# Moving the reload of filter pieces and the first six visits in a fused frequency-filter and feed-forward kernel

## The chip, the cores and the metric

The kernel runs on one core of a Trainium2 chip. The metric is the device time of one execution in microseconds. The engines named here are TensorE (PE in the profile; its weight loads are PEld), VectorE (DVE), ScalarE (ACT), GpSimd (POOL) and SyncE (SP). SP computes nothing; most transfers are issued from its queue (SPq), and the others, mainly loads of the input and of the filter, from GpSimd's.

## The reference

The input x has 8 batches of 3008 positions with 256 channels. The reference multiplies its spectrum along the positions by a complex filter, transforms back, and puts each of the 24064 rows through two matrices with a leaky ReLU between them:

```python
X = np.fft.rfft(x, axis=1)
F = (filt_r + 1j * filt_i)[None, :, :]
y = np.fft.irfft(X * F, n=x.shape[1], axis=1)
h = y.reshape(B * S, D) @ w_in        # 256 x 2048
out = np.maximum(0.01 * h, h) @ w_out # 2048 x 256
```

## The kernel before

**The transform.** 3008 is split as 94 x 32, so the Fourier transform and its inverse are four matmul stages per batch with a turn of the data between stages 1 and 2 (through the DRAM buffer dz1) and between stages 3 and 4 (through dz2). Stage 1 (`s1_group`, L283) makes 16 groups of 512 columns; pairs of them are stored to dz1 (L288) and read back turned (`t1_load`, L297, the z1 loads). Stage 2 transforms and multiplies by the filter; stage 3 transforms back; results are stored to dz2 and read back turned (`t2_load`, L307, the z2 loads); stage 4 (`sb_group`, L461) makes yt, the input of the feed-forward part.

**The filter multiply.** The product of spectrum and filter takes two multiplies by VectorE, one with fb (the imaginary part) and one with fa (the real part), a transfer on SP that exchanges halves or neighbouring partitions of the first product, and an addition on GpSimd. Batches 0 and 1 do it in one layout (`s2_group`, L337 to L352; stage 3 in `sa_group`, L359, with its dz2 store at L363). From batch 2 on (`QUARTERS = 2`) stages 2 and 3 run in tiles of 64 x 64 in so-called visits, six to a batch. A visit (`visit`) calls `forward` for its own part (L411 matmuls, then `filtered` twice, the second time 1.05 slots later: multiplies L421 and L425, two swap copies on SP L424, addition L427) and `backward` for the part of the visit before it (L435 matmuls, ACT copy L437, dz2 store L438). So the addition of one visit has to be done when the next one comes.

**The filter's second layout.** The visits need fa and fb in another order of partitions, so both are loaded again in three pieces by groups: piece 0 holds groups 0 to 11, piece 1 holds 12 to 17, piece 2 holds 18 to 23. A piece cannot be reloaded before batch 1 has used its old content (`when[2, 1, ...]` is the slot of that use). For each piece `refills` issues eight loads on GpSimd (L375, four of fb and four of fa), each filling every other partition, then two copies on SP that fill the neighbours (`both`, L382, fb first) and a sign multiply of fb on VectorE (`signed`, L386). A visit v from 0 to 5 reads groups 2v and 2v + 1 and also 12 + 2v and 13 + 2v: visit 0 needs pieces 0 and 1, visit 3 is the first to need piece 2.

**The feed-forward part.** The rows go in 47 chunks of 512. `moe1` makes the hidden layer of a chunk (L624, with the leaky ReLU on ACT at L629, eight times per chunk). From chunk 3 on the second matrix is applied in seven products instead of eight (`products`, L699), which needs sums on VectorE (L665) and additions of results (L727 to L763); rows are stored from SP (L685).

**Order.** All queues' orders are written out ahead of time. Time in the plan is counted in slots: chunk c takes the slots from 8c to 8c + 8, `at(slot, f)` puts an instruction's issue at a slot, and at the end everything is issued in order of slot. A slot sets only the order within each engine's queue; an engine whose next instruction waits for nothing goes ahead. `PLANS` gives for batches 1 to 4 (later ones repeat batch 4's, shifted) the first slot and step of stage 1, of stage 2, the lag of stage 3, the first slot and step of stage 4, and those of the x loads. A planner loop (L858 to L879) then places each stage's groups at least 0.6 slots apart, away from visits by `AROUND`, and not before their loads can have landed. `load_time` (L839) puts a z1 load at the latest of three: first use less `LEAD[0]` = 3.85 (first use is one slot before the batch's first visit), the end of stage 1 plus 0.53 + 2.43, and 0.1 after the visit that last read its buffer:

```python
loads[stage, b, c] = t = max(first_use[stage, b] - LEAD[stage // 2], place.get((stage, c % 4), 0),
                             when[end] + AFTER[4 * (stage // 2)] + LANDED)
```

In the plan before, batch 1's stage 2 has its groups 5, 8 and 11 at slots 19.67, 24.47 and 28.67, its stage 3 ends at 33.47, and the refills of pieces 0, 1 and 2 begin at 21.37, 26.17 and 46.5. The first four z2 loads of batch 1 are at 36.29, the first eight z1 loads of batch 2 at 40.03, stage 1 of batch 3 runs from 40.7 to 70.85, and the first eight z1 loads of batch 3 are at 73.81. A visit's first swap copies come 0.8 slots after it, the second ones 1.85; its additions are at 1.4 and 2.45.

Of the kernel before, what the change touches and what calls it, by code (L numbers as in the profile page):

```python
# [19 lines left out]
N1, N2 = 94, 32  # L20
# [64 lines left out]
def kernel(  # L85
# [29 lines left out]
    DUE = (3.52, 0.66)  # L115
    TWICE = (2.2, 2.35)
    QUARTERS = 2
    VISITS = (44.75, 49.75, 55.75, 60.75, 65.75, 71.75) + tuple(8 * c + 4.75 for c in range(9, 40))
    AROUND = (0.8, 1.15, 2.1)
    HOLDS = (1.0, 2.0)  # L120
    PAIRS = (0.35, 0.1, 0.1)
# [1 line left out]
    ADDED = 1.4  # L123
    STORED = 1.2
    REFILLED = 1.7
    LATE = 46.5
    F2T = 3.24
    LEAD = (3.85, 7.37)
    AFTER = (0.53, 0.8, 1.33, 3.17, 0.39, 0.52)
# [2 lines left out]
    PLANS = (  # L132
        (0.68, 0.31, 12.95, 0.9, 4.35, 38.33, 2.78, 7.78, 1.61),
        (12.19, 1.53, 42.87, 2.62, 7.4, 85.59, 2.85, 16.13, 2.12),
        (40.7, 1.93, 77.28, 3.57, 5.62, 130.03, 2.65, -0.23, 2.52),
        (63.95, 2.85, 119.86, 3.87, 7.04, 177.42, 2.92, 12.93, 2.24),
    )

# [14 lines left out]
    fa_sb = cpool.tile([P, NC, D], FP16, name="fa_sb")  # L153
    fb_sb = cpool.tile([P, NC, D], FP16, name="fb_sb")
# [38 lines left out]
    def at(time, f):  # L193
        clock["n"] += 1
        heapq.heappush(work, (time, clock["n"], f))
# [8 lines left out]
    def noted(what, f):  # L204
        f()
        issued.add(what)
# [148 lines left out]
    def sa_group(b, g):  # L355
        def go():
            ps = bank("pf", 2, D)
            need(("y", b, g), *[("st2", b, g // 2 - 4)] * (g > 7))
            nc.tensor.matmul(ps, inv2, ys.pop((b, g))[:], start=True, stop=True)  # L359
            h = g // 2  # L360
            nc.scalar.copy(st2[h % 4][:, ds(2 * (g % 2), 2), :], ps)
            if g % 2:
                soon(AFTER[4], lambda: noted(("st2", b, h), lambda: nc.sync.dma_start(  # L363
                    dz2[b % 2][ds(4 * h, 4)].rearrange("k p d -> p k d"), st2[h % 4])))
        return go
# [4 lines left out]
    def halves(v):  # L370
        return v.rearrange("(k e) j d -> e k j d", e=2)

    def refill(dst, src, q, par, k, first, sgn):
        lo = H * par + Q * k
        nc.gpsimd.dma_start(  # L375
            halves(dst[lo : lo + Q, q])[0],
            bass.AP(tensor=src.tensor, offset=src.offset + (first + sgn * (par + 2 * q.start)) * D,
                    ap=[[N1 * D, N2 // 2], [sgn * 2 * D, q.stop - q.start], [1, D]]))

    def both(t, q):  # L380
        v = halves(t[:, q])
        nc.sync.dma_start(v[1], v[0])  # L382

    def signed(q):
        v = fb_sb[:, q]
        nc.vector.tensor_scalar(v, v, sign_sb[:], None, AL.mult)  # L386

    def refills(q, t):
        for n in range(8):
            dst, src = ((fb_sb, filt_i), (fa_sb, filt_r))[n // 4]  # L390
            at(t + 0.4 * n, lambda v=(dst, src, q, n // 2 % 2, n % 2, *((0, 1), (N1, -1))[n % 2]): refill(*v))
        at(t + 4.2, lambda: both(fb_sb, q))
        at(t + 5.6, lambda: both(fa_sb, q))
        at(t + 7, lambda: signed(q))
        if q.start == 0:
            at(t, lambda: nc.sync.dma_start(sign_sb[:], sign_d.ap()))
        elif q.stop < NC:
            t = when[2, 1, 11] + REFILLED
            at(t, lambda: nc.sync.dma_start(i2q_sb[:], i2q_d.ap()))
            at(t, lambda: noted(("f2q",), lambda: nc.sync.dma_start(f2q, f2q_d.ap())))  # L400
# [403 lines left out]
    def plan(b, s1, s1_step, s2, s2_step, lag, sb, sb_step, xl, x_step):  # L804
# [5 lines left out]
        if b < QUARTERS:  # L810
            for g in range(12):
                groups.append((s2 + s2_step * g, 2, b, g, s2_group(b, g)))
                groups.append((s2 + lag + s2_step * g, 3, b, g, sa_group(b, g)))
        first_use[1, b], first_use[3, b] = s2 if b < QUARTERS else VISITS[6 * (b - QUARTERS)] - 1, sb
        for g in range(16):
# [33 lines left out]

    visits = VISITS[: 6 * (B - QUARTERS) + 1]  # L850
    for i, t in enumerate(visits):
# [8 lines left out]
    while queue:  # L860
        time, n, stage, b, g, f = heapq.heappop(queue)
        t = max(time, last + GAP)
        for v in visits:
            if -AROUND[0] < t - v < AROUND[1] or AROUND[1] < t - v < AROUND[2] and last > v:
                t = v + AROUND[1 if last < v else 2]
# [15 lines left out]
    for i, t in enumerate(visits):  # L881
        b, v = QUARTERS + i // 6, i % 6
# [2 lines left out]
            assert ready is not None and ready + READ < t, (b, v, ready, t)  # L885
            place[1, v % 4] = t + 0.1

    for lo, hi, t in ((0, 12, 0), (12, 18, 0), (18, 24, LATE)):
        refills(slice(lo, hi), max(t, when[2, 1, hi // 2 - 1] + REFILLED))

    later = {}
# [49 lines left out]
```

## Time and profile before

| | |
|---|---|
| median of 3 runs | 756.85 us (754.44 to 758.82) |
| profiled execution, its own time | 757.12 us |
| its span from first to last instruction | 755.3 us |
| TensorE busy | 736.3 us (97%) |
| ScalarE busy | 552.4 us (73%) |
| VectorE busy | 527.1 us (70%) |
| GpSimd busy | 180.8 us (24%) |
| mean granted TensorE clock | 0.993 |
| transfers | 117.23 MB, mean 155 GB/s |

The lines of the profile name the engine, the line of the kernel, the operation and its tiles (output, then inputs after the arrow, without buffer numbers). In a timeline the columns are start in us, length in us, engine, line, operation, tiles and forms, the number of instructions merged, and, in square brackets, how long the engine stood idle before and what released it. SPq lines are issues of transfers: their length is that of the issue, not of the transfer. In a table by stretches each engine's busy time is followed by its number of instructions, then come the granted clock (1.00 is full, 0.50 half speed), the mean busy share of the 16 DMA engines and their rate in GB/s.

### The profile page before, as it was taken

The numbers are of one execution on the slowest core, as the hardware profiler recorded it, in microseconds if no ns is written. First come the engines' busy times: TensorE is split into PE (matmuls) and PEld (weight loads), VectorE is DVE, ScalarE is ACT, GpSimd is POOL, SyncE is SP. The second block draws the span as 40 slices with busy tenths as digits, with TensorE's granted clock in tenths as the row PEclk, the third lists the DMA queues.
The fourth block names the chain that finished last, engine by engine and source line by source line (L and its number), as shares of the span: only waits on it lengthen the run. The fifth ranks groups of instructions, "written<-read, shape, count | busy, mean of one in ns | idle before, by whom it ended". The sixth has DMA issues, their size and how long they took to land.

```text
span 755.3 us, 19901 instructions
## 1 busy us (share of the span) xinstructions
PE 736.3 (97%) x8233; PEld 519.6 (69%) x8233; DVE 527.1 (70%) x689; ACT 552.4 (73%) x719; POOL 180.8 (24%) x195
## 2 busy tenths in 40 slices
PE   8999988989999999999999999999999999999997
PEld 3556656656677666777768766786777777777776
DVE  5977635656777777777766777677777778455466
ACT  4776775758877787778778778777777777776762
POOL 5504630433242222222223311221122131000000
PEclk9999999989999999999999999999999999999999
DMA  9997998886687548665576545643364322311012
GB/s 204 227 226 192 226 260 216 181 199 174 194 233 182 153 126 216 177 162 141 153 209 170 156 125 175 188 132 123 105 186 134 122 92 93 107 55 53 30 45 69
DMA packets 124794, 117.23 MB, mean 155 GB/s; under 512 B 17744, under 2 KB 97488, under 8 KB 124512
## 3 DMA queue, kind: packets, MB, share of 16 engines
q1 hardware_dynamic: 105913, 96.72, 41.8%
q0 software_dynamic: 18512, 19.06, 16.8%
q8 instruction: 64, 1.05, 0.6%
q10 hardware_dynamic: 279, 0.19, 0.1%
q14 instruction: 26, 0.21, 0.1%
HBM read 61.07 MB, written 50.33 MB: 147 GB/s over the span
## 4 chain that ended last, share of the span: by engine, by line
PE 91%; DMA 5%; DVE 1%; ACT 1%; issue 0%; POOL 0%; SPq 0%; POOLq 0%; DVEq 0%; ACTq 0%
PE ph L624 42%; PE pf L699 18%; PE po_ps L699 18%; PE pf L283 3%; PE pf L461 3%; PE pf L411 2%; DMA p_b_v<-p_b_v 2%; PE pf L791 1%; PE po_ps L791 1%; PE ph L435 1%; DMA dz<-big 1%; DMA big<-dz 1%; DMA fb_sb<-fb_sb 1%; DMA big<-in_x_dram 1%; PE po_ps L483 1%
## 5 line engine op out<-in xcount | busy, mean ns | idle before, releaser
L629 ACT ACTIVATE gt_c<-ph 128x1024 f16<-128x1024 f32 x376 | 384.9, 1024 | 156.5 <-PE ph L624 152.0
L624 PE MATMUL ph<-yt,w_in_sb 128*128 128x512 f16 (+7 forms) x1728 | 449.5, 353 | 0.2 <-ACT yt L451 0.2
L699 PEld LDWEIGHTS <-gt_c 128*128 128x128 f16 x2800 | 199.1, 98 | 94.3 <-DVE gt_c L665 2.1
L699 PEld LDWEIGHTS <-big 128*128 128x128 f16 x2128 | 146.5, 98 | 70.5 <-issue 14.1
L427 POOL TENSOR_TENSOR y_b_v<-p_b_v,p_b_v 128x512 f16<-128x512 f32 x72 | 103.0, 1431 | 380.8 <-DMA p_b_v<-p_b_v 209.5
L624 PEld LDWEIGHTS <-w_in_sb 128*128 128x128 f16 x1728 | 136.8, 98 | 17.0 <-issue 1.3
L699 PE MATMUL po_ps<-wt_sb,gt_c 128*128 128x128 f16 x704 | 69.2, 219 | 1.9 <-DVE gt_c L665 1.9
L665 DVE TENSOR_TENSOR gt_c<-gt_c 128x2048 f16<-128x2048 f16 x43 | 67.3, 1565 | 1.4
L699 PE MATMUL pf<-wt_sb,big 128*128 128x128 f16 x704 | 66.1, 221 | 1.6 <-DVE big L752 1.6
L699 PE MATMUL pf<-w_out_sb,gt_c 128*128 128x128 f16 x720 | 66.5, 219 | 0.0
L699 PE MATMUL pf<-wt_sb,gt_c 128*128 128x128 f16 x688 | 66.0, 219 | 0.0
L699 PE MATMUL po_ps<-w_out_sb,gt_c 128*128 128x128 f16 x688 | 65.0, 221 | 0.0
L665 DVE TENSOR_TENSOR big<-gt_c 128x2048 f16<-128x2048 f16 (+1 forms) x46 | 64.5, 1402 | 0.3
L286 ACT CAST big<-pf 128x512 f16<-128x512 f32 x98 | 57.0, 583 | 8.7 <-PE pf L283 7.6
L699 PE MATMUL po_ps<-wt_sb,big 128*128 128x128 f16 x688 | 62.9, 219 | 0.0
L451 ACT CAST yt<-pf 128x376 f16<-128x376 f32 x120 | 56.2, 471 | 7.9 <-PE pf L461 5.0
L665 DVE TENSOR_TENSOR big<-big,gt_c 128x2048 f16<-128x2048 f16 (+1 forms) x45 | 56.2, 1249 | 0.1
L421 DVE TENSOR_TENSOR p_b_v<-pf,fb_sb 128x512 f32<-128x512 f32 x72 | 49.3, 685 | 7.7 <-PE pf L411 4.2
L665 DVE TENSOR_TENSOR big<-gt_c,big 128x2048 f16<-128x2048 f16 (+1 forms) x45 | 54.0, 1201 | 0.0
L425 DVE TENSOR_TENSOR p_b_v<-pf,fa_sb 128x512 f32<-128x512 f32 x72 | 48.9, 680 | 0.0
L283 PE MATMUL pf<-x_sb,small_sb 94*128 94x512 f16 x109 | 41.5, 381 | 0.0
L461 PE MATMUL pf<-i_sb,big 96*128 96x94 f16 x448 | 38.4, 207 | 2.4 <-DMA big<-dz 2.4
(108 smaller groups left out, 637.4 us busy)
## 6 DMA issues: line engine op xcount, KB each, us to landing
dz<-big SPq DMA_DIRECT2D x98, 256.0 KB
p_b_v<-p_b_v SPq DMA_DIRECT2D x144, 128.0 KB
out_dram<-ost_c_h SPq DMA_DIRECT2D x118, 128.0 KB
big<-dz SPq DMA_DIRECT2D x56, 192.0 KB
big<-dz SPq DMA_DIRECT2D x72, 128.0 KB
x_sb<-in_x_dram POOLq DMA_DIRECT2D x40, 192.0 KB, 4.8
x_sb<-in_x_dram POOLq DMA_DIRECT2D x2, 768.0 KB, 8.7
big<-dz SPq DMA_DIRECT2D x6, 256.0 KB
```

Of the source, the lines that this page charges most:

```text
L283: nc.tensor.matmul(ps, fwd1[:N1], x_sb[:N1, ds(2 * g, 2), :], start=True, stop=True)
L286: copy(st[:, ds(2 * (g % 2), 2), :], ps)
L411: nc.tensor.matmul(ps[s][ts(par, H), j, :], f2q[ts(s, H), 4 * v + c, :], z1[v % 4][ts(s, H), c, :], start=True, stop=True)
L421: nc.vector.tensor_tensor(p2[:], ps, fb2[:, s, ds(2 * v, 2), :], AL.mult)
L425: nc.vector.tensor_tensor(p1[:], ps, fa2[:, s, ds(2 * v, 2), :], AL.mult)
L427: soon(ADDED, lambda: noted(("yq", b, v, s), lambda: nc.gpsimd.tensor_tensor(y[:], p1[:], p3[:], AL.add)))
L451: copy(yv, ps.rearrange("p c a -> p a c"))
L461: nc.tensor.matmul(ps[:, j, :], z2[h % 4][:K4, j, ts(dt, P)], i1_sb[:K4, 4 * h + j, :], start=True, stop=True)
L624: nc.tensor.matmul(ph[:, j, ds(t - ci * CH, e - t)], w_in_sb[:, dt, ts(ct, P)], yt[:, dt, ds(t % N, e - t)], start=(dt == 0), stop=(dt == ...
L629: nc.scalar.activation(gts[ci][:, ds(2 * g, 2), :], ph, AF.Lrelu)
L665: nc.vector.tensor_tensor(*(v[:, ds(c0, n)] for v in (o, i0, i1)), op)
L699: nc.tensor.matmul(of[t], a()[:, c, ts(t, P)], w[:, c, :], start=(c == 0), stop=(c == NCH - 1))
```

## The change

Four things change, all in the order of work; no instruction is added or taken out.

- `LATE` becomes a tuple with an earliest slot for each of the three filter pieces: 0, 35.5 and 45, where only piece 2 had one, 46.5.
- In `refills` the eight loads of a piece are 0.6 slots apart instead of 0.4, and the two copies and the sign multiply come 7, 8.2 and 11 slots after the first load instead of 4.2, 5.6 and 7.
- The first six visits (batch 2) move from 44.75, 49.75, 55.75, 60.75, 65.75 and 71.75 to 48.75, 53.75, 57.75, 62.75, 67.75 and 71.75. The seventh stays at 76.75.
- The step of batch 3's stage 1 goes from 1.93 to 1.73 slots.

```diff
-    VISITS = (44.75, 49.75, 55.75, 60.75, 65.75, 71.75) + tuple(8 * c + 4.75 for c in range(9, 40))
+    VISITS = (48.75, 53.75, 57.75, 62.75, 67.75, 71.75) + tuple(8 * c + 4.75 for c in range(9, 40))
...
-    LATE = 46.5
+    LATE = (0, 35.5, 45)
...
-        (40.7, 1.93, 77.28, 3.57, 5.62, 130.03, 2.65, -0.23, 2.52),
+        (40.7, 1.73, 77.28, 3.57, 5.62, 130.03, 2.65, -0.23, 2.52),
...
-            at(t + 0.4 * n, lambda v=(dst, src, q, n // 2 % 2, n % 2, *((0, 1), (N1, -1))[n % 2]): refill(*v))
-        at(t + 4.2, lambda: both(fb_sb, q))
-        at(t + 5.6, lambda: both(fa_sb, q))
-        at(t + 7, lambda: signed(q))
+            at(t + 0.6 * n, lambda v=(dst, src, q, n // 2 % 2, n % 2, *((0, 1), (N1, -1))[n % 2]): refill(*v))
+        at(t + 7, lambda: both(fb_sb, q))
+        at(t + 8.2, lambda: both(fa_sb, q))
+        at(t + 11, lambda: signed(q))
...
-    for lo, hi, t in ((0, 12, 0), (12, 18, 0), (18, 24, LATE)):
+    for lo, hi, t in zip((0, 12, 18), (12, 18, 24), LATE):
         refills(slice(lo, hi), max(t, when[2, 1, hi // 2 - 1] + REFILLED))
```

## The prediction

> **What bounds the kernel now.** I read the page's engine rows first, then TensorE's timeline for its idle gaps, then the timelines of VectorE, the DMA queue SP and GpSimd at those gaps, and last a table by stretches for the clock.
>
> ```profile
> PE 736.3 (97%) x8233; PEld 519.6 (69%) x8233; DVE 527.1 (70%) x689; ACT 552.4 (73%) x719; POOL 180.8 (24%) x195
> ```
>
> TensorE is the bound: 97% busy, next 73%. A change that leaves its matmuls alone, as this one does, can move only its idle time and its half-clock time. After the first 35 us TensorE has six gaps over 0.3 us:
>
> ```profile
> 97.49 0.38 PE L359 MATMUL pf<-y_b_g,small_sb 128*128 128x512 f16 x1 [0.48 <-POOL y_b_g L352]
> 101.29 0.38 PE L359 MATMUL pf<-y_b_g,small_sb 128*128 128x512 f16 x1 [0.59 <-POOL y_b_g L352]
> 106.89 0.23 PE L699 MATMUL po_ps<-wt_sb,gt_c 128*128 128x128 f16 x1 [1.95 <-DVE gt_c L665]
> 115.57 0.35 PE L461 MATMUL pf<-i_sb,big 96*128 96x94 f16 x4 [2.36 <-DMA big<-dz]
> 149.72 0.27 PE L699 MATMUL pf<-wt_sb,big 128*128 128x128 f16 x2 [1.62 <-DVE big L752]
> 155.16 0.64 PE L435 MATMUL ph<-y_b_v,i2q_sb 64*64 64x512 f16 x3 [3.14 <-POOL y_b_v L427]
> ```
>
> They add up to 10.14 us, all between 97 and 156 us, the time of filter pieces 1 and 2 and of the first visits. Why they arise stands in the other engines' timelines (VectorE, then SP, then GpSimd):
>
> ```profile
> 105.08 0.62 DVE L386 TENSOR_SCALAR fb_sb<-fb_sb,sign_sb 128x1536 f16<-128x1536 f16 x1 [5.41 <-DMA fb_sb<-fb_sb]
> 148.09 0.97 DVE L386 TENSOR_SCALAR fb_sb<-fb_sb,sign_sb 128x1536 f16<-128x1536 f16 x1 [3.29 <-DMA fb_sb<-fb_sb]
> ```
> ```profile
> 98.60 0.49 SPq L382 DMA_DIRECT2D fb_sb<-fb_sb  x1
> 105.49 1.03 SPq L363 DMA_DIRECT2D dz<-big  x1
> 112.31 1.74 SPq L307 DMA_DIRECT2D big<-dz  x4
> 144.75 0.47 SPq L382 DMA_DIRECT2D fb_sb<-fb_sb  x1
> 148.37 1.17 SPq L424 DMA_DIRECT2D p_b_v<-p_b_v  x2
> 191.64 1.23 SPq L685 DMA_DIRECT2D out_dram<-ost_c_h  x2
> 196.14 5.08 SPq L297 DMA_DIRECT2D big<-dz  x8
> ```
> ```profile
> 153.84 1.26 POOL L427 TENSOR_TENSOR y_b_v<-p_b_v,p_b_v 128x512 f16<-128x512 f32 x1 [4.66 <-DMA p_b_v<-p_b_v]
> ```
>
> VectorE's sign multiply (L386) stood at the head of its queue waiting for the copy of the fb piece, 5.41 and 3.29 us, and the sums and adds behind it, which TensorE needed, came late: gaps 1.95 and 1.62. SP stood at the same copies: the last batch-1 store (L363) went out at 105.49 and the four loads (L307) that need it at 112.31: gap 2.36. At 144.75 SP had waited for piece 2's refill, so the swap copy of visit 1 went out at 148.37 (its product, L421, began at 141.73) and its sum ended at 155.1: gap 3.14. Then the clock (columns: stretch, length, busy time of five engines, granted clock, DMA share, GB/s):
>
> ```profile
> 113.10:116.50 3.40, 1.04 (x14) 0.72 (x13) 0.32 (x1) 1.50 (x2) 0.00 (x0) 1.00 0.94 254
> 116.50:119.90 3.40, 3.40 (x23) 2.42 (x22) 0.56 (x2) 1.50 (x2) 0.00 (x0) 0.50 0.67 194
> 150.60:154.00 3.40, 1.41 (x19) 0.70 (x17) 1.29 (x2) 1.02 (x1) 0.16 (x1) 1.00 0.95 236
> 154.00:157.40 3.40, 2.24 (x13) 1.26 (x13) 1.14 (x2) 1.01 (x1) 2.09 (x3) 0.51 0.72 164
> 157.40:160.90 3.50, 3.50 (x23) 2.37 (x22) 3.02 (x4) 1.66 (x3) 0.00 (x0) 0.50 0.80 201
> ```
>
> After each stretch of 3.4 us with 2 us or more of idle the clock is 0.50, for 3.4 us and for 6.8 us. At half clock half the time is lost: 1.7 and 3.4, together 5.1. So 10.14 + 5.1 = 15.2 us is the most that can be won.
>
> **The change, part by part.** A slot is an eighth of a chunk; from visit 3 to visit 5 of before (167.32 to 189.22 us, 11 slots) a slot took 1.99 us. Queues are in order and run ahead of their slots when nothing holds them.
>
> *Piece 1, from slot 26.17 to 35.5* (copies 42.5 and 43.7, sign 46.5; 30.37, 31.77 and 33.17 before). Taken from its old place: eight refill issues on GpSimd (median 530 ns for fb, 536 for fa, 4.3 us in all), which stood between batch 1's last sums; the two SP copies; the 5.41 us wait of VectorE. Both gaps of L359 (0.48 + 0.59) and the 1.95 go: -3.02. The 2.36: in before the last L359 began at 101.29 and its store at 105.49, 4.2 us later; without the copies on SP I put 1.8 (ACT's copy, 101.70 plus 0.58, then the issue). But GpSimd runs ahead, so the refills are issued at about 101 to 106 us, not slot 35.5, and go on loading the DMA engines while that store lands. I keep 6 us for landing (6.7 before) and 3.2 for the first L307 load: 1.8 + 6 + 3.2 = 11.0 us, against 10.0 us of matmul time between the two points (101.29 to 113.21 less 1.95). One us of the 2.36 stays (bounds 0, and 2.36 if nothing is won): -1.36. With 1 us idle the half clock at 116.5 goes: -1.7. New place: the copy at 42.5 and the sign at 46.5 are 4 slots apart, 8 us; fb copies took 5.85 and 3.3 us. Hidden; if that cover went, VectorE would wait again, up to the 1.95 seen.
>
> *Piece 2, from 46.5 to 45* (copies 52 and 53.2, sign 56; 50.7, 52.1 and 53.5 before). Its fb refills sat behind visit 0's sums on GpSimd; now they are queued ahead of them, and the copy follows the last fb refill by 5.2 slots (10 us) instead of 3. SP's 3.1 us wait for them and VectorE's 3.29 have nothing left to wait for: -1.62, -3.14, and the 3.4 of half clock. The two refills that stood between visit 0's sums (1.07 us at 135.70) also go.
>
> *Piece 0, wider* (copies 28.37 and 29.57, sign 32.37; 25.57, 26.97 and 28.37 before). Same instructions, later; first used at slot 48.75. SP's fa copy waited 2 us for refills, until 92.87; it now stands behind batch 1's last swap copies (slot 29.47). Zero; bounds 0 and 2.
>
> *Visits.* 44.75 to 71.75 becomes 48.75 to 71.75, spacings 5, 4, 5, 5, 4, then 5 to visit 6. Each visit's y must be ready at the next. From a visit's first matmul to the end of its second sum took 9.68 (visit 0), 9.77 (3), 9.93 (4), 10.65 (5), and 7.7 at the quietest (visit 10, 259.29 to 266.99). Four slots are 8.0 us plus 0.24 until L435. Visit 1 to 2: 9.2 (9.68 less about half of the two refills' 1.07) against 8.2: a new wait of 1.0 (bounds 0 by 7.7, 6 by visit 2's 14.2). Visit 4 to 5: 9.93 against 8.4 (visit 4 to 5 was 12.0 us for 6 slots, so 2.0 each, and a store): 1.5 (same bounds). Neither is over the 1.62 that left the clock whole; behind a waiting L435 all of TensorE stands. The three pairs of L624 matmuls held back after a visit (0.35, 0.1 and 0.1 slots) move along: zero. The first eight z1 loads of batch 2 follow, 40.03 to 43.9, 4.85 slots ahead of visit 0 (4.72 before), behind piece 1's copies: zero, at most one copy's 5.85 less the 4 us that a first load has to spare, 2.
>
> *Stage 1 of batch 3, step 1.93 to 1.73.* The same sixteen groups end near slot 66.7 instead of 70.85. Its eight dz1 stores on SP come up to 4 slots earlier, one at a time, and its last x load (slot 60.12, behind visit 2's sum on GpSimd, median 4.8 us to land) still precedes its group (about 65.5): zero for both, 2 us at most if that sum is late. The earlier end frees the first eight z1 loads of batch 3: from 73.81 (bound by stage 1) to 71.9 (visit 6's slot less 1, less 3.85). At 73.81 they stood behind visit 5's swap copies (72.55, 73.6), now ahead of them. They take SP 5.08 us. Visit 5 began at 189.22; its last copy was issued 6.24 us later, SP having stood until 191.64 for an output store. With two loads issued before the visit and six after it (3.8 us), then the store's two, the first copies and a store of batch 2, the last goes out at about 8.3. Sum ready near 12.5 instead of 10.65, visit 6 needs it at 10.4: a wait of 2.0 (bounds 0, and 5 if SP waits for landings too). That is at the edge of what halves the clock (1.62 didn't, 2.0 did): half of 1.7, 0.9. The page "TensorE: Matmul & The Clock Gate" of the Trainium skill (Part 1: The HAM clock gate) says that it falls to half after an idle window of about 3.4 us; the trace shows it after windows idle for 2.36 and 2.0 us, so the measurement decides. By that rule the 0.9 would be nothing and the sum 747.1.
>
> **The sum.** Won: 3.02 + 1.36 + 1.7 + 1.62 + 3.14 + 3.4 = 14.2. Lost: 1.0 + 1.5 + 2.0 + 0.9 = 5.4. Net -8.8 on the profiled execution's own 757.12, 748.3; the median of the runs is 0.27 lower: **748.0**.
>
> **The rivals.** *No new waits.* The spacings suffice (for: 7.7 us at quiet visits and an emptier SP; against: four early visits at 9.7 to 10.7): 757 - 14.2 = 743.
> *The repair is half undone.* Piece 1's transfers, run ahead by GpSimd, keep the z2 wait (2.36 + 1.7 stay, 3.1 of the won lost), and the waits at visits 2 and 5 reach 2 us and cost 1.7 of clock each (1.5 + 3.4 more), 748 + 8 = 756: within 0.5%. For it: DMA share was 0.9 to 1.1 there; against: SP is emptier.
> *Slower: the sum of a visit is late at visits 2, 5 and 6, each with two half-clock stretches.* One mechanism, y latency over spacing. Each wait w then costs w + 3.4. It decides against the change from 3(w + 3.4) = 14.2 + 3.8, so w = 2.6, that is a latency of 10.8 at four slots. At visit 6's 13.4, w is about 5 at visits 2 and 5 and 3 at visit 6: 23 lost, 766. For it: 17.2, 14.2 and 13.4 at visits 1, 2 and 6; against: the first two have the refills as cause, and visit 6 its z1 loads.
>
> **How the numbers follow.** Chances: forecast 0.45 (own range 745 to 752), no new waits 0.22, half undone 0.21, slower 0.12. A measurement of this kernel can tell about 0.5%, 3.8 us (its runs spread by 4.4). Faster: 0.45 + 0.22 + 0.06 of the half undone (below 753) = 0.73; same 0.15; slower 0.12. The range takes in the no-wait case at 741 and the half undone at 758; the slower case is out.
>
> **What would show it.** Right: L386 without a DMA wait at all three pieces; the L363 store within 2.5 us of the last L359; clock 1.00 from 97 to 150 us; visit 1's swap copies issued within 5 us of its first matmul; small L435 gaps at visits 2 and 5; L297 x8 ahead of visit 5's L424, and a gap at visit 6. Wrong: L435 gaps over 2.6 us with 0.50 behind them, or L461 still waiting 2 us for its load.

## The result, and the profile after

The changed kernel takes 760.43 us (median of 20 runs, 756.26 to 763.06) against 755.18 us for the kernel before on the same chips: 1.0064 times, 95% interval 1.0047 to 1.0080. By that ratio it is slower by 4.8 us (the medians lie 5.25 apart) where 8.8 us of gain were forecast from the 756.85 of the first three runs. Its profiled execution has a span of 759.5 us, 4.2 more than before.

TensorE's gaps after the first 35 us are now these (timeline of TensorE, the changed kernel; the last number is the idle time and what ended it):

```profile
113.50 0.50 PE L461 MATMUL pf<-i_sb,big 96*128 96x94 f16 x4 [4.83 <-DMA big<-dz]
145.19 0.41 PE L435 MATMUL ph<-y_b_v,i2q_sb 64*64 64x512 f16 x3 [0.56 <-POOL y_b_v L427]
155.94 0.58 PE L435 MATMUL ph<-y_b_v,i2q_sb 64*64 64x512 f16 x1 [2.70 <-POOL y_b_v L427]
157.71 0.64 PE L435 MATMUL ph<-y_b_v,i2q_sb 64*64 64x512 f16 x3 [1.19 <-POOL y_b_v L427]
182.50 0.41 PE L435 MATMUL ph<-y_b_v,i2q_sb 64*64 64x512 f16 x3 [1.90 <-POOL y_b_v L427]
204.19 0.41 PE L435 MATMUL ph<-y_b_v,i2q_sb 64*64 64x512 f16 x3 [1.48 <-POOL y_b_v L427]
```

The old gaps ahead of L359 and L699 are gone, so the change does what it says. But the gap ahead of L461 has doubled, and every other gap now stands ahead of L435, where a visit waits for the sum of the one before. They add up to 12.66 us (10.14 before). The clock went with them (table by stretches, the changed kernel):

```profile
111.30:118.10 6.80, 4.60 (x33) 3.50 (x34) 0.43 (x1) 1.61 (x3) 0.00 (x0) 0.50 0.75 223
155.70:162.50 6.80, 5.37 (x32) 3.33 (x32) 2.75 (x4) 2.02 (x3) 4.12 (x6) 0.50 0.78 165
183.00:186.40 3.40, 3.40 (x21) 2.14 (x20) 1.96 (x4) 1.46 (x2) 1.26 (x1) 0.50 0.82 174
```

That is 17.0 us of half clock against 10.2. The page gives what the slower matmuls cost:

```profile
PE 739.5 (97%) x8233; PEld 521.4 (69%) x8233; DVE 526.5 (69%) x689; ACT 552.2 (73%) x719; POOL 179.4 (24%) x195
```

TensorE is busy 3.2 us longer with the same 8233 matmuls (736.3 before). With 2.5 us more of gaps, less a gap of 1.47 us at 6.6 us that only the profile of before has, that makes the 4.2 of the spans.

Where the time is lost shows in three matmuls of the hidden layer (L624), counted from the start. The 109th begins at 85.8 us (86.6 before), the 181st at 122.6 (123.9) and the 361st at 213.7 (209.5); from there on the distance stays. So the stretch that holds piece 1's old place and the gap ahead of L461 took 36.8 us against 37.3, and the stretch that holds the first visits 91.1 against 85.6. In this execution all of the loss is at the visits.

For the first gap, GpSimd, then SP (timelines, the changed kernel):

```profile
98.15 2.68 POOL L375 DMA_DIRECT2D fb_sb<-in_filt_i_dram  x4
100.81 1.08 POOL L375 DMA_DIRECT2D fa_sb<-in_filt_r_dram  x2
104.95 1.02 POOL L375 DMA_DIRECT2D fa_sb<-in_filt_r_dram  x2 [0.70 <-DMA x_sb<-in_x_dram]
```
```profile
101.15 0.99 SPq L363 DMA_DIRECT2D dz<-big  x1
110.87 1.74 SPq L307 DMA_DIRECT2D big<-dz  x4
```

Piece 1's loads, planned at slot 35.5, were issued at 98 to 106 us, as nothing ahead of them in GpSimd's queue held them back (the waits in between are 1.83 and 0.70 us). The last dz2 store was issued 4.3 us earlier than before (101.15 against 105.49), but the loads that need it could follow only 9.72 us later (6.82 before): the store came earlier and the wait became longer. TensorE, which no longer stood at L359 and L699, reached this point 4.5 us earlier. So its gap grew, although L461 itself begins 2.1 us earlier than before (113.50 against 115.57).

For the visits, SP between visits 0 and 2 (timeline, the changed kernel; visit 1's first matmul is at 144.01):

```profile
141.61 2.41 SPq L685 DMA_DIRECT2D out_dram<-ost_c_h  x3
144.20 0.54 SPq L382 DMA_DIRECT2D fb_sb<-fb_sb  x1
144.83 0.53 SPq L307 DMA_DIRECT2D big<-dz  x1
145.55 0.53 SPq L382 DMA_DIRECT2D fa_sb<-fa_sb  x1
146.18 0.54 SPq L288 DMA_DIRECT2D dz<-big  x1
146.81 1.86 SPq L297 DMA_DIRECT2D big<-dz  x2
148.77 1.22 SPq L424 DMA_DIRECT2D p_b_v<-p_b_v  x2
```

SP is busy issuing, one transfer after another, from 141.6 to 148.7 us. Visit 1's first swap copy goes out 4.8 us after its first matmul (1.2 at visit 10, a quiet one), its second sum ends at 157.66, 13.65 us after (7.7 at visit 10), and visit 2 came four slots later. The other half of the delay lies behind the issue (GpSimd, then the table by stretches, for visit 1 and for visit 10):

```profile
154.63 1.26 POOL L427 TENSOR_TENSOR y_b_v<-p_b_v,p_b_v 128x512 f16<-128x512 f32 x1 [8.50 <-DVE p_b_v L425]
```
```profile
148.70:154.60 5.90, 4.55 (x55) 3.09 (x54) 5.20 (x7) 4.37 (x7) 0.00 (x0) 1.00 1.00 294
264.70:267.60 2.90, 2.90 (x34) 1.99 (x32) 2.28 (x4) 2.08 (x4) 0.00 (x0) 1.00 0.42 136
```

Visit 1's first sum begins 5.9 us after its first swap copy was issued (2.9 at visit 10), and all that time the DMA engines are busy (share 1.00, against 0.42). The line names a VectorE multiply of visit 2 that ended at that moment; in four of the experiments below (piece 1's loads left out, GpSimd held, piece 1 back, z1 loads put back) the same sum is released by the landing of the copies, 5.7 to 6.5 us after their issue. So against visit 10, visit 1 lost about 3.6 us ahead of the issue and 3.0 in the landing (the rest of its path was 0.6 shorter).

### The profile page after: what moved, and what is told of

Its sections match the earlier page's. It is cut to its first block, busy times and chain, and to the rows that moved or that the text cites. A ratio compares the mean times of both kernels' runs of the same rounds, so it can differ in the third digit from the quotient of the medians.

```text
span 759.5 us, 19901 instructions
## 1 busy us (share of the span) xinstructions
PE 739.5 (97%) x8233; PEld 521.4 (69%) x8233; DVE 526.5 (69%) x689; ACT 552.2 (73%) x719; POOL 179.4 (24%) x195
## 4 chain that ended last, share of the span: by engine, by line
PE 92%; DMA 2%; DVE 2%; POOL 1%; ACT 1%; issue 1%; SPq 1%; DVEq 0%; POOLq 0%; ACTq 0%
PE ph L624 42%; PE pf L699 18%; PE po_ps L699 18%; PE pf L283 3%; PE pf L461 3%; PE pf L411 1%; PE pf L791 1%; PE po_ps L483 1%; PE po_ps L791 1%; DMA dz<-big 1%; PE ph L435 1%; POOL y_b_v L427 1%; DMA p_b_v<-p_b_v 1%; ACT yt L451 0%; PE pf L337 0%
## 5 line engine op out<-in xcount | busy, mean ns | idle before, releaser
L629 ACT ACTIVATE gt_c<-ph 128x1024 f16<-128x1024 f32 x376 | 385.6, 1026 | 153.3 <-PE ph L624 148.7
L624 PE MATMUL ph<-yt,w_in_sb 128*128 128x512 f16 (+7 forms) x1728 | 450.3, 353 | 0.2 <-ACT yt L451 0.2
L699 PEld LDWEIGHTS <-gt_c 128*128 128x128 f16 x2800 | 199.1, 98 | 92.7 <-issue 2.7
L699 PEld LDWEIGHTS <-big 128*128 128x128 f16 x2128 | 147.4, 98 | 68.3 <-issue 12.0
L427 POOL TENSOR_TENSOR y_b_v<-p_b_v,p_b_v 128x512 f16<-128x512 f32 x72 | 101.0, 1402 | 384.7 <-DMA p_b_v<-p_b_v 183.3
L624 PEld LDWEIGHTS <-w_in_sb 128*128 128x128 f16 x1728 | 137.3, 98 | 16.7 <-DVE yt L451 0.4
L665 DVE TENSOR_TENSOR gt_c<-gt_c 128x2048 f16<-128x2048 f16 x43 | 69.1, 1608 | 1.4
L699 PE MATMUL po_ps<-wt_sb,gt_c 128*128 128x128 f16 x704 | 69.8, 221 | 0.0
L699 PE MATMUL pf<-wt_sb,big 128*128 128x128 f16 x704 | 66.6, 222 | 0.0
L699 PE MATMUL pf<-wt_sb,gt_c 128*128 128x128 f16 x688 | 66.2, 219 | 0.0
L699 PE MATMUL pf<-w_out_sb,gt_c 128*128 128x128 f16 x720 | 66.1, 219 | 0.0
L699 PE MATMUL po_ps<-w_out_sb,gt_c 128*128 128x128 f16 x688 | 64.8, 221 | 0.0
L451 ACT CAST yt<-pf 128x376 f16<-128x376 f32 x120 | 56.1, 471 | 10.9 <-PE pf L461 8.1
L699 PE MATMUL po_ps<-wt_sb,big 128*128 128x128 f16 x688 | 63.4, 219 | 0.0
L665 DVE TENSOR_TENSOR big<-big,gt_c 128x2048 f16<-128x2048 f16 (+1 forms) x45 | 53.6, 1191 | 0.1
L437 ACT CAST big<-ph 128x1024 f16<-128x1024 f32 x36 | 36.3, 1007 | 9.8 <-PE ph L435 9.8
L461 PE MATMUL pf<-i_sb,big 96*128 96x94 f16 x448 | 38.6, 208 | 4.8 <-DMA big<-dz 4.8
```

What stands on the lines that cost most here:

```text
L427: soon(ADDED, lambda: noted(("yq", b, v, s), lambda: nc.gpsimd.tensor_tensor(y[:], p1[:], p3[:], AL.add)))
L437: nc.scalar.copy(st2[v % 4].rearrange("p (j w) d -> p w j d", w=2), ps.rearrange("p w (j d) -> p w j d", j=2))
L451: copy(yv, ps.rearrange("p c a -> p a c"))
L461: nc.tensor.matmul(ps[:, j, :], z2[h % 4][:K4, j, ts(dt, P)], i1_sb[:K4, 4 * h + j, :], start=True, stop=True)
L624: nc.tensor.matmul(ph[:, j, ds(t - ci * CH, e - t)], w_in_sb[:, dt, ts(ct, P)], yt[:, dt, ds(t % N, e - t)], start=(dt == 0), stop=(dt == ...
L629: nc.scalar.activation(gts[ci][:, ds(2 * g, 2), :], ph, AF.Lrelu)
```

## The experiments

Two theories were set against each other for each place. *Early gap:* piece 1's loads, run ahead, slow the store (A), or SP's own traffic does (B). *Visits:* four slots are too short (C), or the swap copies are late whatever the spacing (D). Ratios are to the kernel before, run on the same chip, with 95% intervals.

**The loads of piece 1 left out.**

```diff
-        for n in range(8):
+        for n in range(8 if q.start != 12 else 0):
```

> The changed kernel without the eight loads of filter piece 1 (its groups 12 to 17 keep old content; the copies and the sign multiply stay). Theory: GpSimd runs ahead and issues these loads at 98 to 106 us, and their small packets slow the dz2 store that was issued at 101.15 and landed only at about 110.8. Then the store lands in 5 to 7 us, the 4.83 us gap ahead of L461 falls to under 2 us, the half clock from 111.3 to 118.1 us shrinks to 3.4 us or nothing, and the kernel is 4 to 7 us faster than the changed one, at 753 to 756 us. Rival: the store is slow by SP's own traffic (the f2q load and the stores of batches 1 and 2): the gap stays over 4 us and the time within 1.5 us of the changed kernel's 760.4.

Measured: 757.18 us, 1.0021 (0.9996 to 1.0046), 0.43% or 3.2 us less than the change. Timeline of TensorE, then of SP:

```profile
111.86 0.35 PE L461 MATMUL pf<-i_sb,big 96*128 96x94 f16 x4 [2.76 <-DMA big<-dz]
```
```profile
101.14 2.34 SPq L363 DMA_DIRECT2D dz<-big  x1
109.15 1.74 SPq L307 DMA_DIRECT2D big<-dz  x4
```

The gap falls from 4.83 to 2.76 us, but not under 2, and the half clock to 3.4 us; from store to load 8.0 us remain. So leaving the loads out takes away 1.7 of the 2.9 us that were added: A is right in kind and B keeps a share. The L435 gaps at visits 1 and 2 stay (0.87, 3.00 and 1.39 us).

**GpSimd held until the first z2 load has landed.**

```diff
+    held_until = cpool.tile([P, 4], FP16, name="held_until")
...
+        if q.start == 12:
+            at(38.6, lambda: nc.gpsimd.tensor_copy(held_until[:K4], z2[0][:K4, 0, 0:4]))
...
-            at(t + 0.6 * n, ...
+            at(38.7 + 0.3 * n if q.start == 12 else t + 0.6 * n, ...
```

> The changed kernel with GpSimd held: at slot 38.6 it copies four elements per partition of the first z2 load of batch 1, so the eight loads of piece 1 (now at 38.7 to 40.8, copies and sign where the change has them) cannot be issued before that load has landed. Theory: with their packets out of the way the last dz2 store lands within 7 us of its issue instead of 9.7, the gap ahead of L461 falls from 4.83 to 1.5 to 3 us and the half clock there to 3.4 us; that is 3 to 4 us, but the fb copy now waits on SP for the loads and the z1 loads of batch 2 stand behind it, which may cost as much at visit 0: 756 to 760 us, with the first gap shorter in any case. Rival: the store is slow whatever GpSimd does: the gap stays over 4 us.

Measured: 757.74 us, 1.0025 (0.9998 to 1.0051), 0.39% or 2.9 us less than the change. Timelines of SP and of TensorE (L465 is the change's L461, L415 its L411):

```profile
100.41 1.21 SPq L363 DMA_DIRECT2D dz<-big  x1
107.20 1.74 SPq L307 DMA_DIRECT2D big<-dz  x4
```
```profile
110.35 0.35 PE L465 MATMUL pf<-i_sb,big 96*128 96x94 f16 x4 [1.54 <-DMA big<-dz]
130.06 0.30 PE L415 MATMUL pf<-big,f_sb 64*64 64x256 f16 x2 [1.03 <-DMA big<-dz]
131.47 0.41 PE L415 MATMUL pf<-big,f_sb 64*64 64x256 f16 x6 [1.11 <-DMA big<-dz]
```

From store to load it is 6.8 us, as before the change, and no half clock follows the 1.54. This also held one x load that stands among piece 1's loads on GpSimd, which may be the rest that the first experiment left; that was not separated. Of all kernels run, this one reaches the 181st L624 earliest, at 117.3 us. The price shows at visit 0, whose z1 loads are now late (2.1 us in two gaps, 3.4 us of half clock), and the gaps at visits 2, 4 and 6 stay (3.43, 1.83 and 1.85 us).

**Piece 1 back at its old slot.**

```diff
-    LATE = (0, 35.5, 45)
+    LATE = (0, 0, 45)
```

> The changed kernel with piece 1 back at slot 26.17 (steps, visits, piece 2 and stage 1 as changed). Theory: the loads of piece 1 are over before batch 1's last dz2 store is issued, the gap ahead of L461 falls from 4.83 to the 2.3 us of the kernel with wide steps alone, and the 6.8 us of half clock behind it go: 3 to 5 us faster than the changed kernel, 755 to 757.5 us. Rival: the early loads bring back the late sums and the waiting sign multiply (gaps ahead of L359 and L699 of 2 to 3 us together), and the time stays within 1.5 us of the changed kernel's.

Measured: 757.93 us, 1.0019 (1.0003 to 1.0035): piece 1's new slot costs 0.45% or 3.4 us of the change's loss. The gap ahead of L461 was 3.53 us with 3.4 us of half clock, and a gap of 1.15 us stood ahead of an L359. That is the trade of gaps that the theory has, though the one ahead of L461 stayed larger than 2.3. But this profile does not show the gain there: the 181st L624 begins at 122.9 us, no earlier than in the changed kernel (122.6). The two part at the visits, 88.1 us against 91.1 from the 181st to the 361st. Why the visits are better off with the early piece 1 was not tested.

**The wider steps alone.**

```diff
-            at(t + 0.4 * n, ...
-        at(t + 4.2, lambda: both(fb_sb, q))
-        at(t + 5.6, lambda: both(fa_sb, q))
-        at(t + 7, lambda: signed(q))
+            at(t + 0.6 * n, ...
+        at(t + 7, lambda: both(fb_sb, q))
+        at(t + 8.2, lambda: both(fa_sb, q))
+        at(t + 11, lambda: signed(q))
```

> The kernel before with the wider steps of the reload alone (loads 0.6 slots apart, copies at 7 and 8.2, sign at 11; old slots of the pieces, old visits, old stage 1). Theory: L386 no longer waits for its copy (5.41 and 3.29 us before), SP no longer stands for piece 2's loads ahead of visit 1's swap copies; the gaps of 1.95, 1.62 and 3.14 us go, and with them the 6.8 us of half clock: 747 to 751 us. Rival: the copies only move into other work, among them the swap copies of visit 1 or 2, and a gap of 2 to 3 us ahead of L435 stays: 753 to 757 us.

Measured: 751.26 us, 0.9956 (0.9936 to 0.9976): faster than both kernels. L386 waits no more at piece 2, and 1.97 us instead of 5.41 at piece 1. Timeline of SP at the early gap:

```profile
101.62 0.87 SPq L363 DMA_DIRECT2D dz<-big  x1
110.90 1.74 SPq L307 DMA_DIRECT2D big<-dz  x4
```

Here too it is 9.3 us from store to load, although the last of piece 1's loads was issued at 97.3, four us ahead of the store. So a store that goes out at 101 us waits about as long without these loads placed on top of it. Piece 1's copies and loads of x were on their way at that time; which of them counts was not tested. The gap ahead of L461 is only 2.29 us here, because TensorE came to it later.

**The wider steps for piece 2 alone** (each of the four times takes its new value only where `q.stop == NC`).

> The kernel before with the wider steps for piece 2 alone. Theory: the gain of the wider steps lies in piece 2: its copy no longer holds SP ahead of visit 1's swap copies and its sign multiply no longer holds VectorE, so the gaps of 1.62 and 3.14 us and the 6.8 us of half clock at 154 us shrink to one stretch at most; the gaps before 120 us stay: 751 to 754 us. Rival: the gain lies in piece 1 (its late sign multiply behind the 1.95 us gap): then this kernel is within 1.5 us of before.

Measured: 751.68 us, 0.9947 (0.9925 to 0.9969). Timeline of TensorE:

```profile
101.39 0.38 PE L359 MATMUL pf<-y_b_g,small_sb 128*128 128x512 f16 x1 [1.25 <-POOL y_b_g L352]
106.95 0.23 PE L699 MATMUL po_ps<-wt_sb,gt_c 128*128 128x128 f16 x1 [1.91 <-DVE gt_c L665]
115.58 0.35 PE L461 MATMUL pf<-i_sb,big 96*128 96x94 f16 x4 [2.31 <-DMA big<-dz]
151.93 0.41 PE L435 MATMUL ph<-y_b_v,i2q_sb 64*64 64x512 f16 x3 [1.50 <-POOL y_b_v L427]
```

The early gaps are those of before, the gap of 1.62 is gone, 3.14 has become 1.50, and no half clock follows. So, as a time, piece 2 alone wins as much as all three pieces. With all three widened the 1.95 goes, and 1.22 us ahead of a stage-1 matmul (L283) and two gaps at visit 1 (0.78 and 1.93) come.

**Stage 1 of batch 3 at 1.73 alone** (the one line of `PLANS`).

> The kernel before with batch 3's stage 1 at a step of 1.73 alone, which puts its first eight z1 loads at slot 71.9, ahead of visit 5's swap copies, instead of 73.81. Theory of the prediction: visit 5's last swap copy goes out 2 us later, visit 6's L435 waits 1.5 to 2.5 us, half clock with a chance of a half: 757 to 760 us. Rival: the five slots to visit 6 have room for it, and no gap of over 0.5 us arises at visit 6: within 1 us of before.

Measured: 757.73 us, 1.0028 (1.0000 to 1.0056). Timeline of TensorE at visit 6:

```profile
197.87 0.37 PE L435 MATMUL ph<-y_b_v,i2q_sb 64*64 64x512 f16 x1 [0.68 <-POOL y_b_v L427]
199.79 0.41 PE L435 MATMUL ph<-y_b_v,i2q_sb 64*64 64x512 f16 x3 [1.55 <-POOL y_b_v L427]
```

A wait of 2.2 us where there was none. But the same execution also waited 5.37 us at visit 2 (3.14 before) with 6.8 us of half clock, and only 0.48 us ahead of L461 (2.36 before), so its time says little of visit 6.

**The z1 loads of batch 3 put back behind visit 5's copies, in the changed kernel.**

```diff
+            if (stage, b) == (1, 3) and c < 4:
+                loads[stage, b, c] = t = max(t, 73.81)
```

> The changed kernel with the first eight z1 loads of batch 3 at slot 73.81, behind visit 5's swap copies, instead of 71.9; nothing else moves. Theory of the prediction: visit 5's last swap copy goes out 2 to 3 us earlier than now (8.8 us after the visit's first matmul), and the 1.48 us gap at visit 6 goes: 1.5 to 2.5 us faster than the changed kernel, 758 to 759 us. Rival: the loads then stand ahead of visit 6, its operand is late, and a gap at visit 6 or 7 takes its place: within 1 us of the changed kernel.

Measured: 759.65 us, 1.0062 (1.0039 to 1.0086). The gap at visit 6 went from 1.48 to nothing and visit 5's last swap copy from 8.8 to 6.3 us after its first matmul, but the time is within the rival's 1 us. The place is settled, its price in the changed kernel is not: the other gaps of this execution were larger (5.20 ahead of L461, 3.36 at visit 2).

**The new visits, with the step of 1.73, and the filter as before.** With the old step of 1.93 visits that lie closer would push stage 1 back until batch 3's z1 loads came too late for visit 6, so the step belongs to the visits.

> The kernel before with the new visits and the step of 1.73 that they need (with 1.93 stage 1 of batch 3 ends too late for visit 6), but with the filter pieces at their old slots and steps. Theory: the gaps before 120 us stay as before (0.48, 0.59, 1.95, 2.36 and 3.4 us of half clock), and the closer visits bring L435 gaps of 1 to 3 us at visits 2, 5 and 6 with half clock at some of them, in place of the 1.62 and 3.14 of before: 756 to 762 us. Rival: the new visits are harmless or a gain by themselves, and the loss of the changed kernel comes from the pieces' new times: 748 to 753 us.

Measured: 759.55 us, 1.0061 (1.0038 to 1.0083). Timeline of TensorE at the visits:

```profile
154.21 0.58 PE L435 MATMUL ph<-y_b_v,i2q_sb 64*64 64x512 f16 x1 [2.69 <-POOL y_b_v L427]
155.97 0.64 PE L435 MATMUL ph<-y_b_v,i2q_sb 64*64 64x512 f16 x3 [1.18 <-POOL y_b_v L427]
179.85 0.41 PE L435 MATMUL ph<-y_b_v,i2q_sb 64*64 64x512 f16 x3 [1.38 <-POOL y_b_v L427]
199.87 0.41 PE L435 MATMUL ph<-y_b_v,i2q_sb 64*64 64x512 f16 x3 [1.40 <-POOL y_b_v L427]
```

The gaps of the changed kernel at visits 2, 4 and 6, within 0.6 us each, with the filter pieces in their old places. They come from the visits and the step. Piece 2's copies have both been issued here by 142.8 us, when visit 1 begins (142.7). Visit 1's first swap copy goes out 3.5 us after the first matmul (4.8 in the changed kernel), its first sum begins 6.7 us later, and its latency is 13.2 us all the same.

**Visits five slots apart, the rest as changed.**

```diff
-    VISITS = (48.75, 53.75, 57.75, 62.75, 67.75, 71.75)
+    VISITS = (46.75, 51.75, 56.75, 61.75, 66.75, 71.75)
```

> The changed kernel with visits at 46.75, 51.75, 56.75, 61.75 and 66.75, so that each is five slots from the next. Theory one (the four-slot spacings are what hurts): the L435 gaps at visits 2 (0.56 to 2.70 and 1.19) and 5 (1.90) fall to under 1 us each, with 3 to 5 us of half-clock loss gone: 753 to 757 us. Theory two (SP issues too much between visits, and its swap copies go out 3 to 8 us late whatever the spacing): gaps of 2 us or more stay at two or more visits, latencies stay at 11 us and over, and the time is 757 to 761 us.

Measured: 759.31 us, 1.0053 (1.0035 to 1.0070). Timeline of VectorE at visit 0, then TensorE from there:

```profile
135.54 0.62 DVE L386 TENSOR_SCALAR fb_sb<-fb_sb,sign_sb 128x1536 f16<-128x1536 f16 x1 [4.71 <-DMA fb_sb<-fb_sb]
```
```profile
137.41 0.59 PE L283 MATMUL pf<-x_sb,small_sb 94*128 94x512 f16 x1 [3.16 <-DVE p_b_v L425]
158.27 0.41 PE L435 MATMUL ph<-y_b_v,i2q_sb 64*64 64x512 f16 x3 [0.41 <-POOL y_b_v L427]
```

C is right for visits 2 to 5: of the gaps there (2.70 and 1.19 at visit 2, 1.90 at visit 4) 0.41 us is left, and the latencies of visits 1 to 4 are 8.4 to 10.9 us (12.0 to 17.4 in the changed kernel). The time is no better because visit 0 now stands where piece 1 is not ready: VectorE waits 4.71 us for its copy, TensorE 3.16, with 6.8 us of half clock behind. At visit 6 gaps of 0.58 and 1.53 us stay. A late piece 1 needs a late visit 0, and with a late visit 0 there are not five slots for each visit up to visit 6.

**Three attempts to go on from the wider steps.**

```diff
-            place[1, v % 4] = t + 0.1
+            place[1, v % 4] = t + 2.0
```

> The kernel before with the wider steps and, beyond the change, with the two z1 loads that follow each visit placed 2.0 slots after it, behind its swap copies, instead of 0.1, ahead of them. Theory (visits are late because SP issues one transfer per 0.6 us and others stand ahead of the swap copies): every visit's swap copies go out about 1.2 us earlier, visit 0's at 4.4 us after its first matmul instead of 5.7, the gaps of 0.78 and 1.93 us at visit 1 fall to under 1.5 together and its half clock goes: 747.5 to 750 us. Rival: the swap copies wait for landings or for bandwidth, not for SP's issue: within 1 us of the 751.3 us of the wider steps alone.

Measured: 752.08 us, 0.9950 (0.9931 to 0.9969). Visit 0's swap copies went out from 1.5 us after the first matmul instead of 5.7, and the gaps at visit 1 are gone, but gaps of 0.54 and 1.39 us came at visit 3, 0.79 at an L461, and the gap ahead of the first L461 was 3.44 us in this execution. As a time it is the rival's "within 1 us".

With `LATE = 45` besides:

> The kernel before with the wider steps, the two z1 loads behind each visit's swap copies, and piece 2 at slot 45 as in the change, so that its loads are queued on GpSimd ahead of visit 0's sums. Theory: the two loads that stood between visit 0's sums are gone (1.07 us) and the copies are over before visit 2: the gaps at visits 1 to 3 fall under 1 us each: 747 to 750 us. Rival: the earlier loads slow the z1 loads of visit 0 and 1 on the DMA engines: 751 to 754 us.

Measured: 751.85 us, 0.9943 (0.9918 to 0.9968). Gaps at visits 1 and 2 are gone, 1.40 us stays at visit 3; its profiled span, 748.8 us, is the shortest of all, but as a time it is not told apart from the wider steps alone.

With the wider steps and visit 1 at 50.75:

> The kernel before with the wider steps and visit 1 at 50.75 instead of 49.75, six slots behind visit 0. Theory: the gaps of 0.78 and 1.93 us at visit 1 and the 3.4 us of half clock behind them go; visit 2 then comes five slots later, its gap stays under 1.5 us: 747 to 750 us. Rival: the wait moves to visit 2, with its half clock: 750 to 753 us.

Measured: 754.44 us, 0.9971 (0.9951 to 0.9991). The wait moved to visit 2 (0.99 and 2.37 us, and half clock): the rival in kind, and somewhat over its range. The profiled execution also had 3.75 us ahead of L461 with 6.8 us of half clock, some 35 us ahead of the moved visit.

**What the parts add up to.** Relative to before: the wider steps -0.44%, the step of 1.73 +0.28%, the visits on top of it +0.33% (1.0061 less 1.0028), piece 1's slot +0.45% (1.0064 less 1.0019). The sum is +0.62%, measured +0.64%. Each of these ratios is known to 0.2 or 0.3%, so the sum is uncertain by about 0.4%; that it meets the measured value this closely is luck, and a share of piece 2's slot of that size would not be seen.

**The same stretches in every profile.** One execution each, in us:

| kernel | 109th to 181st L624 | 181st to 361st |
|---|---|---|
| before | 37.3 | 85.6 |
| changed | 36.8 | 91.1 |
| changed, piece 1's loads left out | 34.2 | 90.8 |
| changed, GpSimd held | 31.3 | 93.0 |
| changed, piece 1 at its old slot | 36.8 | 88.1 |
| changed, visits five slots apart | 37.4 | 88.0 |
| changed, z1 loads put back | 37.3 | 87.9 |
| wider steps alone | 33.6 | 83.6 |
| wider steps for piece 2 alone | 37.4 | 80.6 |
| step of 1.73 alone | 35.1 | 88.5 |
| new visits and the step | 34.6 | 88.1 |

In the first stretch four kernels have the same filter times (before, piece 2 alone, the step, the visits), and they differ by up to 2.8 us, with gaps of 0.48 to 2.36 us ahead of L461. The wider steps alone and the three attempts from there spread from 33.6 to 38.2. So differences of 3 to 4 us in one execution show nothing, and only the kernel with GpSimd held stands out. The three with piece 1 late and nothing else done to it (36.8 to 37.4) are not told apart from before. In the second stretch all kernels with the new visits or the step take 2 us or more longer than before.

## Why the prediction was wrong, by its own steps

*Piece 1 off its old place.* The two gaps ahead of L359 and the 1.95 went, as forecast (3.02 us). The store did go out sooner, 2.3 us after the last L359 began (1.8 forecast). That SP stood at piece 1's copies, as the prediction reads the profile, has little support: SP's waits for filter loads in before are 3.6 us (fb) and 3.1 us (fa) in all, of which the prediction itself places 3.1 at piece 2 and 2 at piece 0, so that at most 1.6 us is left for piece 1.

*"I keep 6 us for landing".* This step failed. The run-ahead of GpSimd had been seen and timed (98 to 106 us against "about 101 to 106"), but the landing was left shorter than the 6.7 us of before, although the loads were now being placed on top of it and the store was to go out earlier. From issue to the next load it took 9.7. The gap became 4.83 instead of 1.0 and the half clock 6.8 us instead of none: 3.8 + 3.4, 7.2 us off. In place of the 6.1 us won (3.02 + 1.36 + 1.7) the stretch from the 109th to the 181st L624 became 0.5 us shorter: what TensorE no longer lost at L359 and L699 it lost ahead of L461. The loads are a part of the cause (without them 8.0 us, with GpSimd held 6.8), but not all of it, as the 9.3 us of the wider steps alone show. The experiments give piece 1's slot, as a time, 3.4 us of loss; where that arises stays open.

*Piece 2.* Both old gaps went and visit 1's sum no longer waits behind piece 2's loads. The cause read from the profile (SP and VectorE standing at a copy whose loads were late) was right: alone it gives 4.0 us (0.53%), against 8.2 in the sum, since a wait of 1.50 us stays at visit 2 and the rest of the gain is not found in the time. Two sizes were too large: the profile of before was of an execution 1.9 us above the median of 20 runs, and the 5.1 us for half clock takes half of whole stretches, of which 1.16 us was idle that the gaps already count, 0.6 us too much.

*The visits' y latency: 9.2 and 9.93 us.* This is the step that failed and cost most: from the 181st to the 361st L624 it is 5.5 us more, where the terms of the sum have 2.8 less (8.2 won, 5.4 lost). The values were those of visits five and six slots apart with SP nearly free at their start. In the changed kernel visit 1 took 13.65 us, then visits 2 and 3 17.35 and 12.84 behind the stall. Compared with a quiet visit, visit 1 lost about as much ahead of its swap copies, where SP was issuing other transfers, as in their landing, while the DMA engines were full; so latency is not independent of what is placed around the visit. Piece 2's copies in the way are not needed for it, as the experiment with the new visits and the old filter times shows. That full DMA engines make the landing slow fits the profiles (share 1.00 here and 1.03 in that experiment, while the copies landed), but no run varied it alone. Visit 2 waited 2.70 + 1.19 with 6.8 us of half clock (forecast 1.0 and none); the wait forecast for visit 5 did not come, but one of 1.90 at visit 4 with 3.4 us of half clock did.

*Stage 1 at 1.73.* The mechanism was right: eight L297 ahead of visit 5's copies, the last copy 8.8 us after the first matmul (8.3 forecast), a wait at visit 6 of 1.48 + 0.21 (2.0 forecast). Its price as a time is not settled: the step alone is +0.28% (1.0000 to 1.0056), and taking the wait away from the changed kernel won nothing that can be told.

*The rivals.* The one that happened is the half undone repair, in both of its parts (with visit 4 in place of 5), together with the slower one's mechanism at visit 2. They had been treated as different cases with 0.33 between them, and the range left the slower one out; its upper end, 758, lies under the 760.4 measured. The tighter visits and the late piece 1 are one decision, and the profile of before showed that the visits next to filter traffic, 1 and 2, had 17.2 and 14.2 us of latency, not 9.7.

## What to carry to other kernels

A slot in a written-out order holds back only what waits for something: before moving a transfer later, ask what its engine does just ahead of it, and if nothing there waits, it will be issued at once, among whatever was critical at that time. When work is pushed into fewer slots, take latencies from the places with the most traffic and let them grow with the density, rather than from places like the old spacing. And when a change has several parts, run them alone: here one part, piece 2's later copies and sign, is worth 0.5%, and the other parts give back more than that. And read a gap together with a fixed point behind it: a gap that grows because TensorE arrives sooner has cost nothing yet.

## What the runs showed of the hardware

In each of the 14 profiled executions the stretches of half clock begin at whole multiples of 3.41 us from each other. Cut into stretches by that grid (40 to 700 us), every stretch at full clock with 1.83 us or more of TensorE idle was followed by half clock (26 of 26), and none with 1.48 or less was; of the 12 between them two were (1.50 and 1.67) and ten were not (up to 1.82). A stretch at half clock that was itself idle for 1.1 us or more was followed by another one (11 of 11), and one without idle by full clock (28 of 28), which is why half clock lasted 6.8 us in some places and 3.4 in others. So a wait of 1.9 us inside one stretch costs more than itself, while the 1.95 us ahead of L699 in the kernel before, split 1.31 and 0.64 by the grid, cost only itself. The page "TensorE: Matmul & The Clock Gate" of the Trainium skill (Part 1: The HAM clock gate) has the free-running stretch of 3.4 us, which agrees with the 3.41 here, and asks for an idle one before the clock falls; by these traces a little more than half of it idle is enough.
